# Token pairs in the q, k, v loads, no K copy, and an order planned around port and instruction fetch, in a one-core gated DeltaNet and MLP kernel

The kernel runs on one core of a Trainium2 chip. The metric is the device time of one execution in microseconds (us). Executions of the kernel before spread over some 3% on each chip, so every kernel was timed in alternation with it on the same chip. A ratio below is the mean time of one kernel's fast runs over the mean time of the other's fast runs of the same rounds, so it is not quite the ratio of the medians that stand beside it. "Fast" means no more here than within 1.5% of the fastest run that it was compared with.

## The reference

A gated delta rule over 768 tokens for 4 x 8 heads of 48 elements, then an MLP with a smooth ReLU on 3,072 tokens:

```python
def _attn_ref(q, k, v, beta, g):                    # (4, 8, 768, 48); beta (4, 8, 768)
    k_n = k / (np.linalg.norm(k, axis=-1, keepdims=True) + 1e-06)
    state = np.zeros((B, H, D, D))
    for t in range(S):
        y[:, :, t] = g[:, :, t] * np.einsum('bhd,bhde->bhe', q[:, :, t], state)
        v_old = np.einsum('bhde,bhd->bhe', state, k_n[:, :, t])
        state = state + beta_t * np.einsum('bhd,bhe->bhde', k_n[:, :, t], v[:, :, t] - v_old)
    return y

def _moe_ref(x, w_in, w_out):                       # (3072, 384), (384, 2048), (2048, 384)
    h = x @ w_in
    g = np.where(h >= 1, h, np.where(h <= -1, 0.0, (h + 1) ** 2 / 4))
    return g @ w_out
```

## The kernel before

Tokens are taken in 24 steps of 32, and four steps make a **group**. A group is prepared as a whole: load K, q and V; norm and scale; transpose on TensorE (PE); "grams" (K times K and q); mask; invert 128 small triangular matrices ("lanes": 14 rounds of two small operations); two merges. Then its four steps run one after another, each ending with a state update, and the finished group goes through the MLP. All instructions are first listed with an estimated duration and a priority. A planner simulates the engines and emits each engine's instructions in the order of its simulated start times.

```python
class Plan:
    def order(self):                      # a list scheduler with estimated durations
        ...
            if o["dma"] and not o["dma"][0]:
                done = end + 2.5          # a DMA with estimate 0 lands 2.5 us after its issue
        ...
        return [i for t, i in sorted(out)]
    def emit(self):
        for i in self.order():
            self.ops[i]["fn"]()
```

The parts that the change touches:

```python
def load(nm, g, prio, parts, ...):        # one token (192 B) per packet, 128 tokens on 128 partitions
    ... dma_start(out=t(g)[:, a:a + n], in_=whole(src, g, a, n)) ...
def beta_load():                          # 32 heads x 6 groups x 32 tokens: 768 pieces of 128 B
    a = bass.AP(..., ap=[[S, NH], [GS * C, NG], [1, C]])
def load_weights(prio):                   # input weights (win) in 16 pieces of 32 or 16 rows
    ... nc.gpsimd.dma_start(out=win[32 * h4 + p0:32 * h4 + p0 + n, kt, :], in_=moe_w_in[r0:r0 + n, :]) ...
def prep(g, ...):                         # K scaled into k, then copied beside V into pk
    ... tensor_tensor(out=ks(g)...) ... tensor_copy(out=spot(pk, D, a, n), in_=ks(g)...) ...
# order of work
lanes(g, t0 + 1.8 * T, ["POOL"] if g > 1 else ["DVE", "POOL"] if g else ["DVE"])
# (cut: merges, chain_step, mlp_in, mlp_out)
```

Of the kernel before, what the change touches and what calls it, by code (L numbers as in the profile page):

```python
# [22 lines left out]
class Plan:  # L23
# [8 lines left out]
    def add(self, eng, us, fn, r=(), w=(), prio=0.0, ninstr=0, dma=None, take=None, give=None, after=(), soon=0.0):  # L32
# [15 lines left out]
        self.ops.append(dict(eng=eng, us=us, fn=fn, deps=deps, prio=prio, n=ninstr, dma=dma, take=take, give=give, soon=soon))  # L48
        return i

    def order(self):
# [8 lines left out]
        fetch = [0, 0.0]  # L60
        dma = 0.0
# [16 lines left out]
        while len(out) < len(ops):  # L78
# [23 lines left out]
            p, i = heapq.heappop(now)  # L102
            o = ops[i]
            if o["take"]:
                c = o["take"][0]
                most, rest = self.limits[c]
                if held[c] >= most or len(spare) <= rest:
                    blocked.append((e, i))
                    continue
                held[c] += 1  # L110
                self.slot[o["take"]] = spare.pop(0)
            end = t + o["us"]
            if o["n"]:
# [36 lines left out]
def kernel(  # L150
# [17 lines left out]
    DM = H * D  # L168
    J = 8
# [5 lines left out]
    KW = 2 * D  # L175
    assert D == 48 and H == 8 and B == 4
# [17 lines left out]
    kraw = Ring("kraw", 1, [128, NH, D], FP)  # L194
    vraw = Ring("vraw", 1, [128, NH, D], FP)
    qraw = Ring("qraw", 1, [128, NH, D], FP)
    gs = Ring("g", 8, [128, J, D], FP)
    ksq = Ring("ksq", 1, [128, NH, D], FP)
    nsq, nrm, nre, rcp, rs = (Ring(n, 2, [128, NH], FP) for n in ("nsq", "nrm", "nre", "rcp", "rs"))
    ks = Ring("k", 1, [128, NH, 64], F16)  # L200
    qs = Ring("q", 1, [128, NH, 64], F16)
    pks = Ring("pk", 2, [128, 4, J, KW], F16)
# [3 lines left out]
    lts = Ring("lt", 1, [128, 32, 32], F16)  # L206
# [15 lines left out]
    gts = Ring("gt", 20, [128, NT], F16)  # L222
# [3 lines left out]
    sb = pool.tile([128, NG, NH], FP, name="sb")  # L226
# [20 lines left out]
    braw = pool.tile([128, NG, 32], FP, name="braw")  # L247
    bt = pool.tile([128, NG, NH], FP, name="bt")
# [10 lines left out]
    def P(eng, us, fn, r=(), w=(), prio=0.0, ninstr=0, dma=None, take=None, give=None, after=(), soon=0.0):  # L259
        plan.add(eng, us, fn, r, w, prio, ninstr, dma, take, give, after, soon)  # L260

    def whole(t, g, a=0, n=NH):

        return bass.AP(tensor=t.tensor, offset=t.offset + g * GS * C * D + a * S * D, ap=[[D, GS * C], [S * D, n], [1, D]])

    def load(nm, g, prio, parts, eng="SP", after=(), soon=0.0):
        t, src = dict(k=(kraw, k), q=(qraw, q), v=(vraw, v))[nm]
        e = {"SP": nc.sync, "ACT": nc.scalar}[eng]
        for a, n in parts:
            P(eng, 0.5, lambda a=a, n=n: e.dma_start(out=t(g)[:, a:a + n], in_=whole(src, g, a, n)),  # L270
              w=[t.key(g, a)], prio=prio, dma=(5.6 * n / NH, 128 * n), after=after, soon=soon)

    def load_g(s, prio, soon):
        for h4 in range(4):
            a = bass.AP(tensor=g_in.tensor, offset=g_in.offset + (2 * (h4 % 2) + h4 // 2) * S * D + s * C * D,
# [4 lines left out]
    def beta_load():  # L280
        for qd in range(4):
            a = bass.AP(tensor=beta.tensor, offset=beta.offset + qd * C, ap=[[S, NH], [GS * C, NG], [1, C]])
            P("ACT", 0.62, lambda p=32 * qd, a=a: nc.scalar.dma_start(out=braw[p:p + 32, :, :], in_=a),
              w=[("braw", qd)], prio=-120, dma=(0.0, 192))
# [5 lines left out]
    def setup():  # L290
# [13 lines left out]
        P("POOL", 1.9, diag, r=["ones"], w=["id32", "upf", "i128"], prio=-99)  # L304
        for rg in (ks, qs):
            for i in range(rg.n):
                P("DVE", 0.3, lambda i=i, rg=rg: nc.vector.memset(rg(i)[:, :, D:64], 0.0), w=[rg.key(i, "pad")], prio=-98)
        P("POOL", 0.9, lambda: nc.gpsimd.memset(lowl(0)[:], 0.0), w=[lowl.key(0, 0), lowl.key(0, 1)], prio=-40)
        P("POOL", 0.9, lambda: nc.gpsimd.memset(lowx(0)[:], 0.0), w=[lowx.key(0, 0), lowx.key(0, 1)], prio=-40)
# [7 lines left out]
        P("DVE", 0.4, lambda: nc.vector.transpose(out=bt[:].rearrange("p a b -> p (a b)"), in_=braw[:].rearrange("p a b -> p (a b)")),  # L317
          r=[("braw", n) for n in range(4)], w=["bt"], prio=-118)
        P("ACT", 0.36, lambda: nc.scalar.activation(out=sb[:].rearrange("p a b -> p (a b)"), in_=bt[:].rearrange("p a b -> p (a b)"), func=AF.Sqrt),
          r=["bt"], w=["sb"], prio=-118)  # L320

    def fill_bm(i, after=()):
# [3 lines left out]
        P("POOL", 2.7, f, r=["id32"], w=[bms.key(i, c) for c in range(GS)], prio=-55 + 20 * i, after=after)  # L326

    WIN = [("win", h4, kt, p0) for h4 in range(4) for p0, kt in ((0, 0), (0, 1), (16, 1), (0, 2))]

    def load_weights(prio):  # L330
        wp = win[:].ap[0][0]
        for h4 in range(4):
            for p0, kt, h2, e0, n in ((0, 0, 0, 0, 32), (0, 1, 0, 32, 16), (16, 1, 1, 0, 16), (0, 2, 1, 16, 32)):
                r0 = (h2 * 4 + 2 * (h4 % 2) + h4 // 2) * D + e0
# [84 lines left out]
    def ktk(g):  # L419
        return [kts.key(g, j) for j in range(J)]  # L420
# [304 lines left out]
```

## Time and profile before

| kernel before | |
|---|---|
| time, median of 4 runs beside the changed kernel | 335.99 us (332.31 to 341.31) |
| profiled run | 334.0 us, PE busy 242.6 us |
| first state update / that of step 4 / first MLP matmul | 44.3 / 93.8 / 91.3 us |
| PE idle before the first MLP matmul / after it | 58.0 / 33.3 us |

The shares of the engines and the busy time by stretch stand in the prediction. Two more views. First, the DMA view of the kernel before, from 0 to 20 us: 40 slices of 0.5 us, busy share of the 16 DMA engines in tenths, then GB/s.

```profile
DMA  0000999999999999997399999999999997000000
GB/s 0 0 0 17 200 256 252 184 200 243 250 198 252 245 218 214 237 233 122 66 224 261 255 193 249 244 238 235 219 216 218 218 218 113 0 0 0 0 0 0
```

From 2 to 17 us nearly all DMA engines work, mostly at 180 to 260 GB/s, with one dent to 66 GB/s. Second, two rows of the timeline of the kernel before, DVE and then PE; the brackets give the idle time before an instruction and what ended it.

```profile
7.41 0.38 DVE L317 STREAM_TRANSPOSE bt<-braw 128x192 f32<-128x192 f32 x1 [3.59 <-DMA braw<-in_beta_dram]
```
```profile
37.81 0.91 PE L498 MATMUL psn_158<-l_105,bm_97 32*32 32x32 f16 x52 [13.20 <-DVE l_105 L479]
```

Beta is there at 7.4 us, and the first merges start at 37.8 us, when DVE has inverted group 0.

### The profile page before, as it was taken

What the parts mean: (1) busy time and instruction counts of PE and PEld (TensorE: products, weight loads), DVE (VectorE), ACT (ScalarE), POOL (GpSimd) and SP (SyncE); (2) the same over time, 40 slices, a digit from 0 to 9 for tenths busy, and PEclk for the clock granted to TensorE, in tenths of its full rate; (3) what the DMA queues carried; (4) which work ended last, traced back from release to release, by engine and by line L of the source; (5) the groups of instructions that cost most, each with busy time, mean ns of one, the idle gap of its engine ahead of it and who ended that gap; (6) DMA issues with size and microseconds to landing.
All of it is one profiled execution on the core that took longest, in us unless ns stands there. A gap on an engine that the chain in (4) does not pass through costs nothing.

```text
span 334.0 us, 15565 instructions
## 1 busy us (share of the span) xinstructions
PE 242.6 (73%) x6960; PEld 149.6 (45%) x6960; DVE 212.9 (64%) x371; ACT 173.8 (52%) x300; POOL 165.7 (50%) x271
## 2 busy tenths in 40 slices
PE   0250364307678859797595997898997999899985
PEld 0140363206544436454363554555554555455443
DVE  3899922777677793774654676747538571985570
ACT  3430152004575637755386636587363764876871
POOL 8596091272625895478574158822485220332330
PEclk9999999999995878999669899589997899999999
DMA  8979699773388338645884343022110002001102
GB/s 174 213 135 192 109 162 211 150 154 81 68 160 168 76 69 166 136 108 116 185 167 103 74 113 68 10 69 58 49 49 4 6 3 73 27 3 48 48 0 94
DMA packets 112130, 32.56 MB, mean 97 GB/s; under 512 B 103488, under 2 KB 111680, under 8 KB 112064
## 3 DMA queue, kind: packets, MB, share of 16 engines
q1 hardware_dynamic: 104352, 27.54, 39.1%
q0 software_dynamic: 2752, 3.15, 6.0%
q10 hardware_dynamic: 4960, 0.89, 1.4%
q8 instruction: 54, 0.88, 1.1%
q14 instruction: 12, 0.10, 0.1%
HBM read 25.26 MB, written 4.72 MB: 90 GB/s over the span
## 4 chain that ended last, share of the span: by engine, by line
PE 43%; DVE 20%; POOL 13%; issue 12%; ACT 5%; DMA 4%; ACTq 1%; SPq 1%; DVEq 0%; POOLq 0%
POOL lm_101 L469 5%; POOL tm_102 L466 5%; PE psn_162 L602 3%; DVE lt_100 L447 3%; PE psn_160 L629 3%; PE psn_158 L602 2%; PE psn_159 L602 2%; PE psn_159 L629 2%; PE psn_163 L602 2%; DVE lm_101 L469 2%; DVE tm_102 L466 2%; PE psn_160 L602 2%; DMA out_dram<-ot_151 2%; PE psn_161 L602 2%; PE psn_161 L629 2%
## 5 line engine op out<-in xcount | busy, mean ns | idle before, releaser
L602 PEld LDWEIGHTS <-win 128*128 128x128 f16 x288 | 26.4, 103 | 28.7 <-issue 7.3
L615 POOL TENSOR_TENSOR rl_127<-rl_127 128x512 f32<-128x512 f32 x12 | 12.5, 1040 | 34.1 <-ACT rl_127 L605 34.1
L615 POOL TENSOR_TENSOR rl_126<-rl_126 128x512 f32<-128x512 f32 x12 | 13.2, 1098 | 32.6 <-ACT rl_126 L605 32.6
L469 POOL TENSOR_TENSOR lm_101<-lm_101,tm_102 128x28 f32<-128x28 f32 (+13 forms) x70 | 24.6, 351 | 5.5
L466 POOL TENSOR_TENSOR tm_102<-lt_100,lm_101 128x28 f32<-128x28 f16 (+13 forms) x70 | 23.7, 338 | 5.1
L615 POOL TENSOR_TENSOR rl_128<-rl_128 128x512 f32<-128x512 f32 x12 | 12.9, 1077 | 18.2 <-ACT rl_128 L605 18.2
L457 POOL TENSOR_SCALAR lm_101<-lt_100 128x512 f32<-128x512 f16 (+1 forms) x5 | 6.9, 1385 | 26.8 <-DVE lt_100 L447 21.0
L408 PEld LDWEIGHTS <-k_83 128*128 128x128 f16 x96 | 11.5, 121 | 17.1 <-DVE k_83 L367 16.1
L566 ACT CAST s_120<-sps 128x768 f16<-128x768 f32 x11 | 8.8, 800 | 13.9 <-PE sps L563 13.8
L566 ACT CAST s_119<-sps 128x768 f16<-128x768 f32 x12 | 9.7, 808 | 8.9 <-PE sps L563 8.9
L367 POOL TENSOR_TENSOR k_83<-kraw_61,rs_82 128x768 f16<-128x768 f32 x6 | 8.8, 1484 | 9.9 <-DVE rs_82 L365 9.9
L408 PE MATMUL psn_158<-i_169,k_83 128*128 128x128 f16 x24 | 5.2, 263 | 11.1 <-DVE k_83 L367 10.6
L409 PEld LDWEIGHTS <-q_84 128*128 128x128 f16 x96 | 11.6, 121 | 3.2 <-issue 1.6
L385 POOL CAST q_84<-qraw_63 128x768 f16<-128x768 f32 x10 | 8.7, 880 | 6.5 <-DMA qraw_63<-in_q_dram 6.1
L375 POOL TENSOR_TENSOR pk_85<-vraw_62,sb 128x768 f16<-128x768 f32 x6 | 8.9, 1475 | 4.9 <-DMA vraw_62<-in_v_dram 3.8
L498 PEld LDWEIGHTS <-bm_97 32*32 32x32 f16 x256 | 4.2, 111 | 15.6 <-issue 15.6
L356 ACT ACTIVATE ksq_72<-kraw_61 128x768 f32<-128x768 f32 x12 | 10.0, 840 | 2.4 <-issue 1.5
L501 ACT CAST e_109<-psn_158 128x512 f16<-128x512 f32 x2 | 1.2, 586 | 19.2 <-PE psn_158 L498 19.2
L498 PE MATMUL psn_158<-l_105,bm_97 32*32 32x32 f16 x64 | 1.1, 227 | 13.2 <-DVE l_105 L479 13.2
L367 POOL TENSOR_TENSOR k_83<-kraw_61,rs_81 128x768 f16<-128x768 f32 x4 | 5.9, 1472 | 9.1 <-DVE rs_81 L365 9.1
L602 PE MATMUL psn_162<-xt_124,win 128*128 128x512 f16 x30 | 9.4, 429 | 0.0
L375 POOL TENSOR_TENSOR pk_86<-vraw_62,sb 128x768 f16<-128x768 f32 x6 | 8.9, 1504 | 1.1 <-DMA vraw_62<-in_v_dram 1.1
(591 smaller groups left out, 861.2 us busy)
## 6 DMA issues: line engine op xcount, KB each, us to landing
kraw_61<-in_k_dram SPq DMA_DIRECT2D x12, 384.0 KB, 4.0
qraw_63<-in_q_dram SPq DMA_DIRECT2D x12, 384.0 KB, 6.3
vraw_62<-in_v_dram SPq DMA_DIRECT2D x10, 384.0 KB, 5.8
wout<-in_moe_w_out_dram POOLq DMA_DIRECT2D x4, 384.0 KB, 8.7
out_dram<-ot_151 SPq DMA_DIRECT2D x8, 192.0 KB, 1.9
out_dram<-ot_152 SPq DMA_DIRECT2D x8, 192.0 KB, 1.9
out_dram<-ot_153 SPq DMA_DIRECT2D x8, 192.0 KB, 1.9
win<-in_moe_w_in_dram POOLq DMA_DIRECT2D x8, 128.0 KB, 5.8
```

The lines of the kernel that those rows point to most:

```text
L356: P("ACT", 0.25 + 1.3 * f, lambda hs=hs: nc.scalar.activation(out=ksq(g)[:, hs], in_=kr[:, hs], func=AF.Square), r=[kraw.key(g, a)], w=[ks ...
L367: P(eng, (0.15 + 1.65 * f) if eng == "DVE" else (0.2 + 2.8 * f), lambda hs=hs, a=a, n=n, eng=eng: EW[eng].tensor_tensor(out=ks(g)[:, hs, 0 ...
L375: P(eng, (0.15 + 1.65 * f) if eng == "DVE" else (0.2 + 2.8 * f), lambda hs=hs, a=a, n=n, eng=eng: EW[eng].tensor_tensor(out=spot(pk, 0, a, ...
L408: nc.tensor.matmul(tp[:, hh, 0], kk[:, o:o + 128], i128[:], start=(hh == 0), stop=True, skip_group_check=True)
L409: nc.tensor.matmul(tp[:, hh, 1], qq[:, o:o + 128], i128[:], start=False, stop=True, skip_group_check=True)
L447: P("DVE", 1.95, lambda: nc.vector.transpose(out=lt[:].rearrange("p i j -> p (i j)"), in_=_ap(bm, [[1, 32], [64, 32]])), r=[bms.key(gi, c) ...
L466: e.tensor_tensor(out=tv, in0=_ap(lt, [[528, nb], [32, n], [0, j]], 32 * (j + 1) + j + ot), in1=_ap(lm, [[256, nb], [0, n], [1, j]], 16 * ...
L469: e.tensor_tensor(out=lv, in0=lv, in1=tv, op=ALU.subtract)
L566: P("ACT", 0.8, lambda: nc.scalar.copy(out=s16n[:].rearrange("p a j d -> p a (j d)"), in_=sps[:, :, 0:J * D]), r=["sps"], w=[s16s.key(s)], ...
L602: nc.tensor.matmul(hp, win[:, kt_, m * 128:m * 128 + 128], xt[:, kt_].rearrange("p b t -> p (b t)"), start=(kt_ == 0), stop=(kt_ == 2))
L615: P("POOL", 1.05, lambda: nc.gpsimd.tensor_tensor(out=rl[:], in0=rl[:], in1=rl[:], op=ALU.mult), r=[rls.key(i)], w=[rls.key(i)], prio=prio)
L629: nc.tensor.matmul(bv(n, DM), gts(gi * NM + m)[:, b * GS * C:(b + 1) * GS * C], wout[:, m, :], start=(m == 0), stop=(m == NM - 1))
```

## The change

The intent: a packet of q, k or v carries two neighbouring tokens (384 B instead of 192 B). K is scaled straight into its place beside V, so the copy goes. Group 1's lanes leave DVE. Later groups are prepared up to three steps earlier. The planner keeps VectorE's two-port work apart from GpSimd's, and fills with MLP matmuls where it believes that the next block of instructions is not there yet. Along with that, the input weights are loaded in fewer, larger DMAs and beta in larger packets. The planner's transfer estimate for a whole K, q or V was lowered too, from 5.6 to 3.5 us. The core of the diff:

```diff
+            if e == "PE" and fetch[0] + ops[i]["n"] >= 256 and fetch[1] + 3.4 > t + 0.3:
+                few = [x for x in now if 0 < ops[x[1]]["n"] <= 8 and not self.full(x[1], held, spare)]
+                ...                                   # take the MLP matmul first
+            if o["port"]:
+                end = max(t, port[e == "DVE"]) + o["us"]
+                port[e == "POOL"] = end
 ...
-    kraw = Ring("kraw", 1, [128, NH, D], FP)
+    kraw = Ring("kraw", 1, [128, 2 * J, TP, D], FP)    # TP = 2 tokens
 ...
-            a = bass.AP(tensor=beta.tensor, ..., ap=[[S, NH], [GS * C, NG], [1, C]])
+            a = bass.AP(tensor=beta.tensor, ..., ap=[[0, 2], [2 * S, 2 * J], [1, S - x]])
 ...
-        for h4 in range(4):
-            for p0, kt, h2, e0, n in (...): ...        # 16 input-weight DMAs
+        parts = [(win[:, 0, :], [[D * DFF, 4], [DFF, 32], [1, DFF]], 0, 128), (win[:, 2, :], [[D * DFF, 4], [DFF, 32], [1, DFF]], ..., 128)]
+        for h4 in range(4):
+            parts.append((win[32 * h4:32 * h4 + 32, 1, :], [[160 * DFF, 2], [DFF, 16], [1, DFF]], ..., 32))
 ...
-            P("DVE", ..., tensor_copy(out=spot(pk, D, a, n), in_=ks(g)...))
+                P(eng, ..., lambda: EW[eng].tensor_tensor(out=<K's place in pk>, in0=raw, in1=scale, op=ALU.mult), port=True)
 ...
-        lanes(g, t0 + 1.8 * T, ["POOL"] if g > 1 else ["DVE", "POOL"] if g else ["DVE"])
+        lanes(g, t0 + 1.8 * T, ["POOL"] if g else ["DVE"])
+    PRE = 3.0                                          # groups 2 to 5 prepared 3 steps earlier
```

## The prediction

> **What bounds the kernel now.** I read the page first: the busy shares of the engines, then the span in 40 slices.
>
> ```profile
> PE 242.6 (73%) x6960; PEld 149.6 (45%) x6960; DVE 212.9 (64%) x371; ACT 173.8 (52%) x300; POOL 165.7 (50%) x271
> ...
> PE   0250364307678859797595997898997999899985
> ...
> DMA  8979699773388338645884343022110002001102
> ```
>
> No engine is busy throughout, but the PE row has two halves: poorly filled for about eleven slices, and 70 to 90% and more after. So I asked for the busy time in stretches, cut at 91 us, where the first matmul of the MLP (line 602) stands. The columns are the stretch and its length, then busy time with counts for PE, weight loads, DVE, ACT and POOL, the granted clock, the DMA share and GB/s.
>
> ```profile
> 0.00:91.00 91.00, 32.95 (x1512) 27.99 (x1516) 60.71 (x134) 26.46 (x48) 50.22 (x89) 1.00 0.83 150
> 91.00:334.00 243.00, 209.66 (x5456) 121.63 (x5456) 152.16 (x238) 147.30 (x252) 115.50 (x183) 0.90 0.35 78
> ```
>
> This is the account I shall use: span = PE busy + PE idle. In the first 91 us PE idles 91 - 33 = 58 us; in the other 243 us it idles 33 us. After 91 us PE has the MLP as filler. At the end it even has a stock of it: the last state update (line 563) is at 288 us, and PE runs MLP matmuls almost without a hole until 331 us, when two groups of MLP, about 2 x 21 us, were still to do (16 x 0.65 us on line 602 and as much on line 629, durations from the chain of work). So a shorter recurrence does not by itself shorten the end. What counts is how early PE gets MLP work, and how many holes it has after.
>
> Where do the 58 us go? The timeline of DVE between 12 and 20 us, then POOL in the same time (start, duration, engine, line, operation):
>
> ```profile
> 12.53 3.12 DVE L362 TENSOR_SCALAR nre_77<-nrm_75 128x16 f32<-128x16 f32 x1 [0.28 <-ACT nrm_75 L360]
> ...
> 16.79 2.18 DVE L367 TENSOR_TENSOR k_83<-kraw_61,rs_81 128x768 f16<-128x768 f32 x1
> 19.00 1.11 DVE L370 COPY pk_85<-k_83 128x768 f16<-128x768 f16 x1
> ```
> ```profile
> 12.40 1.48 POOL L375 TENSOR_TENSOR pk_85<-vraw_62,sb 128x768 f16<-128x768 f32 x1 [3.79 <-DMA vraw_62<-in_v_dram]
> 13.82 1.80 POOL L324 MEMSET bm_98<- 128x2048 f16 x1
> ```
>
> The same DVE operations on the first half of K took 0.17, 0.96 and 0.36 us. Here 16 elements take 3.12 us and end exactly when POOL's memset does (15.65 against 15.62). The excess is 2.95 + 0.61 (line 365: 0.78 for 0.17) + 1.22 + 0.75 = 5.5 us, all on the chain.
>
> Then PE's own timeline, the idle time in brackets:
>
> ```profile
> 54.25 0.51 PE L434 MATMUL psn_158<-kt_95 48*32 48x64 f16 x23
> 59.23 0.32 PE L434 MATMUL psn_158<-kt_95 48*32 48x64 f16 x9 [4.47 <-issue]
> ...
> 73.84 0.51 PE L554 MATMUL psn_159<-rr_115,z_112 32*32 32x48 f16 x32 [10.02 <-DVE rr_115 L542]
> ```
>
> The 4.47 us hole lies in the middle of 32 equal matmuls, with nothing to wait for. Counted in the timeline, such holes in mid-block (at 42.01, 46.56, 52.76, 59.23) are 128 matmuls apart, which is 256 instructions with the weight loads: instruction fetch. The page counts 54 instruction packets of 0.88 MB; 13,920 PE instructions over 256 gives the same 54. Up to 91 us the chain of work holds seven such pieces: 1.02 + 1.83 + 1.27 + 4.47 + 0.74 + 2.29 + 0.64 = 12.3 us. The longest falls into the stretch 50 to 60 us, where the DMA share was 1.27. The 10.02 us hole is step 2 waiting for one DVE subtraction, queued behind half of group 1's triangular inverse ("lanes", lines 457 to 475), which ran on DVE from 62 to 73 us. Before that, group 0's lanes took DVE from 27.4 to 36.6 us.
>
> **What the Trainium skill says.** "GPSIMD Engine Reference", Specifications: its SBUF interfaces are shared with VectorE, with contention for DVE instructions in a 2-port mode or with two SBUF inputs. The 3.12 us row agrees; the lanes, with two SBUF inputs each, also stretch from 0.21 to 0.33 us while POOL runs its half. "Runtime: NRT & Kernel Launch", Instruction fetch mechanics: blocks of 16 KiB, 256 instructions, fetched ahead by DMA, the cost "mostly hidden". The block size agrees; mostly hidden it is not here (12.3 us before 91). "DMA: Bandwidth & Descriptors", Specifications: line rate wants at least 512 B. Now q, k, v rows are 192 B each, and the page has 103,488 of 112,130 packets under 512 B at 97 GB/s on average; 384 B is better and still under the mark. "TensorE: Matmul & The Clock Gate", Part 1: 128-column matmuls run 107 ns apart cold and about 56 warm. The trace agrees: line 408 and 409 go every 0.11 us at 47 us and every 0.06 us at 94 us.
>
> **The change part by part.**
>
> Token pairs. A packet carries two tokens. q, k, v need 6 groups x 3 x 4096 = 73,728 packets now, half that after, out of the 104,352 on that queue. The queue's 39.1% share of 334 us is 131 us; if its packets cost alike, 36,864 fewer save 36.9/104.4 x 131 = 46 us of mean DMA time. Almost all is hidden after 91 us; in the start it brings K, then V, a few us earlier and frees the path for instruction fetch. Beta goes from 768 packets to 128; today DVE waits for it until 7.41 us (3.6 us idle).
>
> K copy dropped. Line 370 goes: 12 copies, 5.2 + 3.0 = 8.2 us of DVE; of it 0.36 to 1.11 us in group 0 on the chain. The transposes now read K where it lies beside V, so they wait for V as well, and K needs two 64-column matmuls where one of 128 stood: 16 more per group, 96 in all. If they do not overlap in the array, 96 x 0.055 = 5 us more PE time; I expect some overlap and take 4. Norms go in one piece after group 0, saving about 0.6 us of small DVE operations (lines 362, 364, 365: 0.17 + 0.25 + 0.17) in each of 5 groups, off the path.
>
> Port-aware order. Group 0's K chain should lose nearly all of the 5.5 us. Beta and V earlier, and no issue of V's load on ACT (ACT's squares stood from 8.67 to 10.42 behind it), are worth 2 to 3 us more: step 0, whose first matmul is at 43.0, comes at about 35.
>
> Lanes of group 1 on POOL alone. DVE is free between 62 and 73 us, so steps 1 to 3 do not wait 10 us. The price: POOL needs some 28 x 0.345 + 1.4 + 0.95 + 0.57 = 12.6 us for a whole group (rows of lines 466, 469, 457, 472, 475), so step 4 is set by the path V and K scaling, transposes, grams, lanes, two merges. From 36 us, the earliest that the code allows, with 6 us of POOL scaling, about 4.5 for transposes, 5.5 for grams, masks and the transpose, 13 for lanes, 6 for the rest, that is about 72 us, against 93 now. Steps 0 to 3 need 3.9 us each undisturbed (L554 at 73.84 and 77.68), here with group 1's work between, perhaps 7: from 35 to about 62. First MLP matmul at about **64 us, not 91**.
>
> Fetch-aware order. Where the next block isn't there, MLP matmuls (8 instructions or fewer for 0.65 us) go first. It can only help where MLP exists. After 91 us the chain's pieces of fetch over 0.7 us sum to 1.85 + 0.79 + 1.53 + 0.78 + 2.07 = 7.0; I credit 5. Fewer holes should also leave fewer cold matmuls (triples on line 602 that take 1.39 us for 0.65): credit 3 us of busy time.
>
> Loads and preparation three steps earlier, 19 for 20 MLP buffers, fewer weight DMAs: hidden, 0.
>
> **Sum.** Early idle: by 64 us PE will have done about 28 us of work (the 33 less group 1's merges and the transposes of group 2), so it idles 36 us instead of 58. Late idle: 33 - 5 = 28. Busy: 242.6 + 4 - 3 = 243.6. Together 36 + 28 + 243.6 = 307.6, say **308 us**: 8% off.
>
> **Rivals.** (a) *POOL becomes the bound in the middle.* It takes all lanes of group 1, and three prepared groups at a time compete for it; if group 1's lanes end at 75 us rather than 66, PE uses up MLP group 0 and stands idle until step 7 is done. For it: 58 us busy in 91 to 180 already. Against it: 0.5 of the span in all, and each group's MLP is 21 us of filler. It would cost 8 to 12 us: 318. (b) *The 58 us aren't won because instruction fetch, not data, paces the start.* 54 blocks at a few us each are serial; more matmuls, closer together, wait at each boundary, with no filler before the MLP. For it: 12.3 us today. Against it: DMA is emptier. First MLP then at 74: 318. (c) *The gain is larger.* If PE stays warm in the middle (mean granted clock after 91 us is 0.90, so up to 21 us are there to win) and the late idle falls to 20, the result is near 295. (d) *DMA hidden anyway.* The packets alone would give nearly nothing after 91 us; I count on them only for the start.
>
> **Range and chances.** The sum has 22 us from the early idle (likely 14 to 32), 8 from fetch and clock (0 to 18), -4 for the extra matmuls (-6 to 0). Combined, 295 to 321. The three runs of the kernel before spread from 332.3 to 341.3, so run noise is small beside this. Slower or same needs rivals (a) and (b) both and more: faster by over 2% 0.93, within 0.06, slower 0.01.
>
> **What would show it.** Right: first matmul of the MLP near 64 us; no DVE operation of 16 elements over 0.5 us in the first 20 us; first state update near 36; no 10 us hole at step 2; q, k, v packets halved; PE's idle time before the first MLP about 36 us and after it about 28. Wrong: MLP still starting after 75 us; a PE hole after the first MLP group with POOL's lanes as the releaser; fetch holes in mid-block as long as before; PE busy time above 250 from the 192 half-width K matmuls.

## More of the kernel before

Most kernels have 4 runs, beside few of the kernel before; e8 has 12, and e3, e5, e12, e13 and e17 have 20. Set against all runs of the kernel before that the record calls fast on that chip, the 4-run ratios shift: e1 from 1.028 to 1.037, e16 from 1.045 to 1.056, e18 from 1.023 to 1.034, e15 from 1.011 to 1.006. So differences of about a point are weak where a kernel with 4 runs is one of the two.

## The result, and the profile after

| | before | after |
|---|---|---|
| median (4 runs each) | 335.99 us | 349.75 us (346.20 to 351.24) |
| ratio after to before, 95% interval | | 1.0482 [1.0329, 1.0635] |
| profiled run | 334.0 us | 349.4 us |
| first state update / that of step 4 / first MLP matmul | 44.3 / 93.8 / 91.3 us | 62.3 / 118.5 / 101.0 us |
| PE busy / idle before the first MLP matmul / idle after it | 242.6 / 58.0 / 33.3 us | 242.3 / 71.6 / 35.5 us |

The result is correct and **4.8% slower**, with 308 us predicted. The ratio rests on the two runs of the kernel before that lie within 1.5% of its fastest (332.31 and 334.01 us); over all four the means differ by 3.8%. A repeat on another chip (e16 below) gave 1.0447. From the page of the changed kernel: busy shares, PE and DMA in 40 slices, all packets, then the load queue.

```profile
PE 242.3 (69%) x7056; PEld 150.7 (43%) x7056; DVE 194.6 (56%) x313; ACT 175.8 (50%) x297; POOL 163.5 (47%) x259
...
PE   0027005234376854689897889989898999899986
...
DMA  5569978993897396376740223421321002001102
...
DMA packets 76074, 32.85 MB, mean 94 GB/s; under 512 B 67304, under 2 KB 75496, under 8 KB 76008
...
q1 hardware_dynamic: 71684, 28.52, 41.4%
```

PE's busy time has not changed. It starts one slice later, its fifth and sixth slices are empty, and until the eleventh it is busy for half of a slice or less but for one slice (70%). The queue of the loads has 71,684 packets instead of 104,352, but its share of the span rose: 41.4% of 349.4 us is 145 us of mean DMA time, where it was 131 us. The busy time in two stretches, cut at the first MLP matmul, columns as in the prediction:

```profile
0.00:101.00 101.00, 29.37 (x1272) 25.02 (x1272) 42.56 (x92) 27.16 (x51) 44.29 (x66) 0.91 0.88 148
101.00:349.40 248.40, 212.96 (x5786) 125.71 (x5784) 152.04 (x221) 148.69 (x247) 119.21 (x194) 0.89 0.33 72
```

PE idles 101.0 - 29.4 = 71.6 us in the first stretch, 13.6 us more than before, and 35.4 us in the second, 2.1 more. Together, less 0.3 us of busy time, that is the 15.4 us by which the profiled runs differ. So the loss lies before the first MLP matmul. The DMA view of the changed kernel, 0 to 20 us, in the same slices as before:

```profile
DMA  0000075999999411148995111116999311116997
GB/s 0 0 0 0 25 111 140 302 221 149 194 227 190 76 38 28 38 106 197 297 176 73 26 43 25 55 57 174 255 236 122 44 45 42 41 36 118 253 309 148
```

Three times the DMA engines fall to a tenth of their time and the rate to some 25 to 57 GB/s: from 7 to 8.5, 11 to 13.5 and 16 to 18 us. What then stands still is seen in the timeline of the changed kernel, DVE first, then POOL, then PE:

```profile
17.52 0.25 DVE L341 STREAM_TRANSPOSE bt_164<-braw 128x64 f32<-128x64 f32 x1 [15.16 <-DMA braw<-in_beta_dram]
...
34.74 1.75 DVE L387 TENSOR_REDUCE nsq_74<-ksq_72 128x32 f32<-128x1536 f32 x1 [1.76 <-ACT ksq_72 L385]
36.41 1.89 DVE L483 STREAM_TRANSPOSE lt_99<-bm_96 128x1024 f16<-128x1024 f16 x1
```
```profile
24.43 2.92 POOL L404 TENSOR_TENSOR pk_84<-vraw_62,sb 128x768 f16<-128x768 f32 x2 [16.19 <-DMA vraw_62<-in_v_dram]
...
75.11 1.60 POOL L413 CAST q_83<-qraw_63 128x768 f16<-128x768 f32 x2 [14.67 <-DMA qraw_63<-in_q_dram]
```
```profile
22.30 0.61 PE L437 MATMUL psn_157<-i_169,q_83 128*128 128x128 f16 x4 [22.30 <-ACT q_83 L411]
...
51.74 0.96 PE L534 MATMUL psn_161<-l_105,bm_96 32*32 32x32 f16 x56 [17.71 <-DVE l_105 L515]
...
75.99 0.61 PE L437 MATMUL psn_159<-i_169,q_83 128*128 128x128 f16 x4 [12.71 <-POOL q_83 L413]
```

Three things can be read here. **Beta comes at 17.5 us instead of 7.4**, and V at 24.4 us. **Work of later groups stands in front of earlier work**: at 34.74 DVE reduces the norms of group 1 (nsq_74), having waited for them, before it transposes group 0's masks, which were complete at 33.0 us. At 75.99 PE has waited 12.7 us for the q of group 2, while the matmuls of step 1 stand behind that instruction. And the input weights came late. The list of DMA issues has the size of each and the median time from issue to landing, the kernel before first, then the changed one:

```profile
win<-in_moe_w_in_dram POOLq DMA_DIRECT2D x8, 128.0 KB, 5.8
```
```profile
win<-in_moe_w_in_dram POOLq DMA_DIRECT2D x2, 512.0 KB, 21.0
...
win<-in_moe_w_in_dram POOLq DMA_DIRECT2D x4, 128.0 KB, 20.0
```

Pieces of the same 128 KB took 5.8 us before and 20.0 us after. In the same lists a half of K takes 4.0 us from issue to landing before and 8.1 us after, while the plan assumed less time than before.

### The profile page after: what moved, and what is told of

Read it like the earlier page. It is cut to its first block, busy times and chain, and to the rows that moved or that the text cites.

```text
span 349.4 us, 15681 instructions
## 1 busy us (share of the span) xinstructions
PE 242.3 (69%) x7056; PEld 150.7 (43%) x7056; DVE 194.6 (56%) x313; ACT 175.8 (50%) x297; POOL 163.5 (47%) x259
## 3 DMA queue, kind: packets, MB, share of 16 engines
q1 hardware_dynamic: 71684, 28.52, 41.4%
## 4 chain that ended last, share of the span: by engine, by line
PE 41%; issue 4%; DVE 4%; ACT 4%; DMA 2%; SPq 2%; POOL 1%; DVEq 0%; POOLq 0%; ACTq 0%
PE psn_157 L669 4%; PE psn_162 L669 3%; PE psn_159 L669 3%; PE psn_160 L639 3%; PE psn_158 L639 3%; PE psn_161 L639 2%; PE psn_160 L669 2%; PE psn_161 L669 2%; PE psn_157 L639 2%; PE psn_162 L639 2%; PE psn_159 L639 2%; PE sps L597 2%; SPq L299 1%; PE psn_161 L546 1%; DMA g_70<-in_g_dram 1%
## 5 line engine op out<-in xcount | busy, mean ns | idle before, releaser
L655 POOL TENSOR_TENSOR rl_126<-rl_126 128x512 f32<-128x512 f32 x12 | 12.9, 1078 | 56.9 <-ACT rl_126 L642 56.9
L505 POOL TENSOR_TENSOR lm_101<-lm_101,tm_102 128x28 f32<-128x28 f32 (+6 forms) x70 | 26.0, 372 | 5.5
L437 PEld LDWEIGHTS <-q_83 128*128 128x128 f16 x96 | 8.2, 127 | 36.6 <-ACT q_83 L411 22.3
L655 POOL TENSOR_TENSOR rl_127<-rl_127 128x512 f32<-128x512 f32 x12 | 12.5, 1042 | 22.0 <-ACT rl_127 L642 21.9
L655 POOL TENSOR_TENSOR rl_128<-rl_128 128x512 f32<-128x512 f32 x12 | 12.5, 1041 | 17.1 <-ACT rl_128 L642 17.1
L437 PE MATMUL psn_157<-i_169,q_83 128*128 128x128 f16 x20 | 3.0, 307 | 22.7 <-ACT q_83 L411 22.3
L404 POOL TENSOR_TENSOR pk_85<-vraw_62,sb 128x768 f16<-128x768 f32 x6 | 9.3, 1560 | 15.3 <-DMA vraw_62<-in_v_dram 12.3
L502 POOL TENSOR_TENSOR tm_102<-lt_100,lm_101 128x28 f32<-128x28 f16 (+6 forms) x42 | 14.5, 345 | 2.6
L413 POOL CAST q_83<-qraw_63 128x768 f16<-128x768 f32 x8 | 6.4, 833 | 14.7 <-DMA qraw_63<-in_q_dram 14.7
L385 ACT ACTIVATE ksq_72<-kraw_61 128x1536 f32<-128x1536 f32 (+1 forms) x7 | 9.0, 1295 | 8.2 <-DMA kraw_61<-in_k_dram 8.2
L437 PE MATMUL psn_159<-i_169,q_83 128*128 128x128 f16 x28 | 3.8, 282 | 12.9 <-POOL q_83 L413 12.7
L404 POOL TENSOR_TENSOR pk_85<-kraw_61,rs_82 128x768 f16<-128x768 f32 x6 | 9.5, 1593 | 4.3 <-DVE rs_82 L394 4.3
L502 POOL TENSOR_TENSOR tm_102<-lt_99,lm_101 128x28 f32<-128x28 f16 (+6 forms) x28 | 10.2, 364 | 1.7
L639 PE MATMUL psn_157<-xt_123,win 128*128 128x512 f16 x33 | 10.6, 436 | 0.0
L404 POOL TENSOR_TENSOR pk_84<-kraw_61,rs_81 128x768 f16<-128x768 f32 x4 | 6.4, 1614 | 6.9 <-DVE rs_81 L394 6.8
L341 DVE STREAM_TRANSPOSE bt_164<-braw 128x64 f32<-128x64 f32 x3 | 0.7, 246 | 15.5 <-DMA braw<-in_beta_dram 15.2
```

What stands on the lines that cost most here:

```text
L385: P("ACT", 0.2 + 1.3 * f, lambda js=js: nc.scalar.activation(out=ksq(g)[:, js], in_=kr[:, js], func=AF.Square), r=raw(kraw, g), w=over(ksq ...
L404: P(eng, (0.15 + 1.65 * f) if eng == "DVE" else (0.05 + 2.9 * f), lambda o=o, eng=eng: EW[eng].tensor_tensor(**o()), r=raw(raw_, g) + (ove ...
L413: P("POOL", 0.05 + 1.6 * f, lambda o=o: nc.gpsimd.tensor_copy(**o()), r=raw(qraw, g), w=over(qs.key, a, n), prio=prio)
L437: nc.tensor.matmul(tp[:, x, c], qq[:, c, j * 128:j * 128 + 128], i128[:], start=(x == 0 and c == 0), stop=True, skip_group_check=True)
L502: e.tensor_tensor(out=tv, in0=_ap(lt, [[528, nb], [32, n], [0, j]], 32 * (j + 1) + j + ot), in1=_ap(lm, [[256, nb], [0, n], [1, j]], 16 * ...
L505: e.tensor_tensor(out=lv, in0=lv, in1=tv, op=ALU.subtract)
```

## The experiments

Two theories were formed from this. **N (narrow transfers)**: the Trainium skill, "DMA: Bandwidth & Descriptors", section "Why a DMA increments its semaphore by 16 and not by 1", under "How many engines (k)", says that a DMA is spread over the largest k up to 16 that divides the slowest dimension (that is not 1) of both sides. The new beta pattern has slowest dimension 2, the new weight pieces 4 or 2. The trace agrees: at times when only beta's packets were being moved, 2.1 to 2.2 packets were in flight on average, against about 20 when K was. The new beta is also larger: 64 packets of 3,072 B and 64 of 2,816 B (368 KB), where 768 packets of 128 B were 96 KB. At the 35 to 41 GB/s of those stretches, 368 KB take some 9 to 11 us (an estimate). **Q (queue order)**: each engine's order is that of the planner's estimates, and where these are far off, work of later groups blocks an engine until its data comes. The rivals are those of the prediction (POOL, instruction fetch), and **C**: PE's cold clock gives gains back.

All kernels below give correct results except e4. Two times stand for how far a kernel has come: the first state update (step 0, the first of group 0) and that of step 4 (the first of group 1).

### e1, e2, e3: wide transfers

e1 takes beta with 32 rows as the slowest dimension, e2 the input weights in 16 pieces as before, e3 both. The instruction order of e3 was compared with that of the changed kernel and is the same but for the added DMA issues.

```diff
-            a = bass.AP(tensor=beta.tensor, offset=beta.offset + h4 // 2 * S + x, ap=[[0, 2], [2 * S, 2 * J], [1, S - x]])
+            a = bass.AP(tensor=beta.tensor, offset=beta.offset + x, ap=[[S, NH], [1, S - x]])
 ...
-        parts = [...]                                  # 2 + 4 DMAs, slowest dimension 4 or 2
+            for p0, kt, row, n in ((0, 0, h4 * D, 32), (0, 1, h4 * D + 32, 16), (16, 1, (4 + h4) * D, 16), (0, 2, (4 + h4) * D + 16, 32)):
+                ... out=win[32 * h4 + p0:32 * h4 + p0 + n, kt, :], in_=moe_w_in[row:row + n, :] ...
```

> The changed kernel with one edit: each of the four beta loads takes all 32 heads as 32 rows (slowest dimension 32) instead of 16 rows read twice (slowest dimension 2); the wanted half is picked by the two square roots behind it. Bytes, descriptor sizes and the order of work on every engine stay the same. Theory N (narrow transfers): a transfer whose slowest dimension is 2 runs on 2 of the 16 DMA engines, so beta, 4 x about 92 KB, lands at 17 us; with 32 rows it lands by 8 to 10 us, the first transposes come at 13 to 15 instead of 22.3 us, and the time falls by 6 to 9 us, to 341 to 344. Rival O (order: work of later groups put ahead of its data blocks the engines): the start is paced by K, q and V as before, the time stays within 2 us of 350. Rival P (the 384-byte packets to 64 partitions are slow): beta lands late still, since K and q hold the engines; within 2 us.

> The changed kernel with one edit: the first MLP weight is loaded in 16 pieces of 32 or 16 rows (slowest dimension 32 or 16) instead of 6 pieces whose slowest dimension is 4 or 2. Order of work the same on every engine but for the added issues on POOL. Theory N: those loads land in about 6 us instead of 20, the second group of k/v rows (10.7 us from issue to landing) and the instruction fetches near 42 to 50 us are no longer behind them; gain 3 to 8 us, to 342 to 347. Rivals O and P: the weights are needed at 101 us only, no gain, within 2 us of 350.

> The changed kernel with both edits, wide beta and wide MLP weight. Theory N alone: the whole loss is undone and some of the forecast gain appears, 325 to 336. If N is right but only half of the cause, the hole of 12.7 us on PE before group 2's q transposes (63 to 76 us) stays, since that transfer was issued only at 60.7 us, and the time is 336 to 343: then the order (O) holds the rest. P alone: 348 to 352.

Measured: e1 1.0277 [1.0195, 1.0359], e2 1.0256 [1.0157, 1.0355], e3 1.0177 [1.0135, 1.0219]. The mechanism of N holds: in e1 beta is there at 8.67 us; in e2 weight pieces land in 5.4 us. By the ratios each is worth about 2 points against the 1.048 and 1.045 of the changed kernel, both together about 3. All three times missed what N expected (e3: 344.8 us, not 325 to 336). And e1's gain did not come as N said: its first state update is at 71.6 us, later than the 62.3 of the changed kernel, while steps 1 and 4 are earlier (81.6 for 85.0, 114.7 for 118.5). This is e1's DVE timeline:

```profile
37.32 1.75 DVE L387 TENSOR_REDUCE nsq<-ksq 128x32 f32<-128x1536 f32 x1 [12.55 <-ACT ksq L385]
38.99 1.89 DVE L483 STREAM_TRANSPOSE lt<-bm 128x1024 f16<-128x1024 f16 x1
```

Group 0's masks were complete at 24.8 us, 8 us earlier than in the changed kernel. Yet DVE stood for 12.55 us at the norms of group 1, whose K was issued at 19.3 us and came late beside the narrow weight loads. The transpose of the masks, ready all the time, ran at 38.99, later than the 36.41 of the changed kernel. Q is seen here in one row. The planner, printed by itself, has beta's transpose at 4.54 us (measured 17.5), this reduction at 22.24 and the mask transpose at 23.99 (measured 36.41): in the plan K of group 1 was there in time, and the reduction had the higher priority.

### e4: the narrow transfers in the kernel before

Both kinds of transfer of the kernel before made narrow (the expectation names beta alone), its order otherwise its own. The result is wrong (relative error 0.05), as rows go to other places.

```diff
-            a = bass.AP(..., offset=beta.offset + qd * C, ap=[[S, NH], [GS * C, NG], [1, C]])
+            a = bass.AP(..., offset=beta.offset + qd * C, ap=[[S, 2], [2 * S, 16], [1, NG * C]])
 ...                                                   # and the 2 + 4 weight DMAs of the change
```

> The kernel before with one edit: its four beta loads have the same bytes, in 32 rows of 768 B in the order 2 x 16 (slowest dimension 2) instead of 32 x 6 pieces of 128 B. The result is wrong on purpose. Order of work unchanged. Theory N: beta runs on 2 engines and lands at 11 to 15 us instead of 7.4, the first transposes move by as much, and the time grows by 3 to 8 us, to 338 to 343. Rivals O and P: fewer and larger packets can only help, within 2 us of 335.

Measured: 1.0197 [1.0087, 1.0307]. Slower, as N says, but its trace doesn't show the loss where N puts it. Beta comes at 8.41 us (1 us later), the first state update at 45.2 (0.9 later), step 4 at 96.9 (3.1 later). PE idles 1.4 us more before the first MLP matmul, but 6.7 us more after it, and is 3.6 us longer busy. But this beta is still 96 KB, a quarter of the changed kernel's, so e4 tests a narrow beta without the added bytes; at 35 to 41 GB/s it takes less than 3 us (an estimate). That width and bytes together do harm in an order that is not the changed kernel's, e14 below shows. Where e4's 2% comes from is not settled.

### e5, e6, e7: group 0 first, no early preparation

e5 is e3 with group 1's norms (DVE) and scaling (POOL) ordered behind group 0's lanes. e6 is e3 with PRE = 0. e7 has both.

```diff
-  r=over(ksq.key, a, n), w=over(nsq.key, a, n), prio=prio)
+  r=over(ksq.key, a, n), w=over(nsq.key, a, n), prio=prio, after=[lowx.key(0, 0)] if g == 1 else ())
 ...                                                   # the same after= on the K and V scaling
-    PRE = 3.0
+    PRE = 0.0
```

> Wide loads (as e3) and one change of order: group 1's norm (DVE) and its K and V scaling (POOL) come after group 0's triangular inverse. In e3 DVE stood 5.9 us waiting for group 1's K ahead of group 0's transpose of the masks, then 1.75 us for that norm, and the inverse took 12.4 us beside POOL's scaling against 8.3 before. Theory O (work of later groups put ahead): the first update of the state comes at 52 to 56 instead of 66 us, the first MLP matmul at 82 to 88 instead of 92.5, and the time falls to 332 to 340. Rival F (DMA and fetch bound start): the gained time turns into longer instruction-fetch holes and waits for loads between 45 and 65 us, the time stays at 341 to 346.

> Wide loads (as e3) and PRE = 0: loads and preparation of groups 2 and later are not put three steps earlier in the order. Theory O, second part: group 2's q and K loads no longer share 45 to 65 us with the weights and no longer stand on PE before step 1; steps 1 to 3 come 4 to 8 us earlier and the time falls by 2 to 8 us, to 336 to 342. If early preparation is worth what it was meant to be, later groups are late instead and the time grows to 346 to 352.

> Wide loads with both changes of order (e5 and e6). Theory O: gains add, 326 to 336, faster than the kernel before. Rival F: no better than the better of the two.

Measured: e5 1.0084 [1.0050, 1.0119], e6 1.0468 [1.0387, 1.0549], e7 1.0373 [1.0283, 1.0463]. The first part of Q holds: the first state update moves from 66.0 us (e3) to 48.8, earlier than expected, and about a point is won (343.3 us, not the expected 332 to 340). My suspicion of early preparation as such does not: without it, both kernels lose nearly 3 points. In e5, PE next stands at

```profile
62.89 0.61 PE L437 MATMUL psn<-i,q 128*128 128x128 f16 x4 [6.49 <-POOL q L413]
```

again group 2's q ahead of step 1, whose state update comes only at 69.6 us.

### e8, e11: group 2 behind group 1

e8 is e7 with PE's transposes of later groups placed behind the masks of the group before, and the output weights loaded later. e11 has only the first of the two.

```diff
+              ... take=n, after=[bms.key(g - 1, c) for c in range(GS)] if g > 1 else ())
 ...
-              after=[l16s.key(0)], w=[("wout", i)], ..., soon=38.0)
+              after=[l16s.key(0)], w=[("wout", i)], ..., soon=60.0)
```

> As e7, and two more: group 2 and later transposes on PE only after the group before has its masks, and the second MLP weight (3.1 MB, wanted at about 100 us) is held back to a planned 60 us instead of 38. Theory F: DMA has less to carry between 45 and 65 us, fetch holes there shrink from 3.9 and 5.4 us to under 2.5, time 2 to 6 us under e7. Theory O alone: within 3 us of e7, as the rest of the order is the same.

> e7_g0_first_pre0 (352.8, ratio 1.0373) with only the one order change that PE takes group 2's transposes after group 1's masks; the output weights still load early. Between e7 and e8 3.8 points lie. If blocked PE queue is their cause (Q): ratio 1.00 to 1.01, second state update near 61 instead of 69.8. If the early load of the output weights, which shares DMA with instruction fetch, is the cause: ratio stays above 1.025.

Measured: e8 **0.9995 [0.9947, 1.0043]**, e11 1.0299 [1.0206, 1.0391]. With width and order repaired, the change is as fast as the kernel before. Between e7 and e8 lie 3.8 points; the transposes account for 0.7 and the output weights for the other 3. The same 42 matmuls in PE's timeline, e11 first, then e8:

```profile
62.54 0.77 PE L470 MATMUL psn<-kt 48*32 48x64 f16 x42 [5.42 <-issue]
```
```profile
59.04 0.77 PE L470 MATMUL psn<-kt 48*32 48x64 f16 x42 [3.61 <-issue]
```

With the early load, e11's PE stands 5.42 us in mid-block, without a wait, and then 4.23 us for a K/V transfer at 68.0. In e8 the first wait is still 3.61 us, where under 2.5 was expected, and the second is gone; the first state updates follow at 49.4, 60.9, 67.8 and 72.1 us and the first MLP matmul at 75.4, 16 us earlier than in the kernel before. That these 16 us are worth nothing is taken up below. In e8's DVE timeline, at the start:

```profile
8.40 0.37 DVE L341 STREAM_TRANSPOSE bt<-braw 128x64 f32<-128x64 f32 x2 [6.05 <-DMA braw<-in_beta_dram]
...
14.51 4.53 DVE L404 TENSOR_TENSOR pk<-kraw,rs 128x384 f16<-128x384 f32 x4
```

Even wide and in order, K's scaling ends at 19.0 us, as in the kernel before (16.79 + 2.18): the four operations take 4.53 us, as POOL scales V from 15.28 to 18.63. In the changed kernel, where V was late, the same four took 1.96 us.

### e9, e10, e12, e15: single parts of the change, in the repaired order

Each differs from e8 in one thing: PRE back at 3.0 (e9); group 1's lanes split over DVE and POOL as in the kernel before (e10); the fetch rule off (e12); the port rule off (e15).

```diff
-    PRE = 0.0
+    PRE = 3.0                                                                    # e9
-        lanes(g, t0 + 1.8 * T, ["POOL"] if g else ["DVE"])
+        lanes(g, t0 + 1.8 * T, ["POOL"] if g > 1 else ["DVE", "POOL"] if g else ["DVE"])   # e10
-            if e == "PE" and fetch[0] + ops[i]["n"] >= 256 and ...
+            if False and ...                                                     # e12
-            if o["port"]:
+            if False:                                                            # e15
```

> The kernel of e8_all_order (339.0 us, ratio 0.9995) with early preparation put back (three steps ahead for groups 2 to 5). Theory Q (work of later groups that stands ahead of earlier work in an engine's queue, waiting for its own data, causes the loss): with those blocks now placed after the earlier group's work, early preparation no longer blocks and helps as in e3 against e6 (2.9 points): 330 to 334 us, ratio 0.97 to 0.985. Rival C (the time is set by PE's warm-up and total queue length, early preparation only moves work): no gain, ratio 0.99 to 1.01. First state updates in both: 49, 61, 68, 72.

> e8_all_order with group 1's triangular inverse split again, one half on DVE and one on POOL, as in the kernel before. Rival (a) of the prediction (POOL bounds the middle): e8's step 4 (94.8 us) comes at about 86 and the ratio falls from 0.9995 to about 0.98. Theory Q: step 4 comes earlier, but MLP of group 0 fills PE meanwhile and DVE delays steps 1 to 3: within 0.5 per cent of e8.

> e8_all_order without the rule that puts MLP matmuls ahead where the planner believes that the next instruction block is not there. The prediction credited the rule with 5 us of idle and 3 of clock (2.4 per cent): then 347, ratio 1.02. Theory Q has nothing on it; the planner's block times (3.4 us each) seldom hit the real holes, so I expect within 0.7 per cent of e8.

> e8_all_order with the planner no longer keeping POOL work and DVE's two-port work apart. The prediction valued that at 5.5 us in the start: then step 0 comes about 4 to 6 us later and the ratio is 1.01 to 1.02. Rival: in e8's trace the K scaling on DVE already runs beside POOL's V scaling (4.53 us for 1.96), so the rule holds only in the plan, not on the chip: within 0.7 per cent of e8.

Measured: e9 1.0201 [1.0141, 1.0260], e10 1.0233 [1.0148, 1.0318], e12 1.0039 [1.0004, 1.0073], e15 1.0111 [1.0056, 1.0166].

- e9 missed its expectation of 0.97 to 0.985. At 79.2 us PE again waits 5.59 us for a later group's K scaling on POOL, step 4 comes at 105.3 instead of 94.8. Early preparation helped e3 and hurts e8, so these edits do not add up.
- e10: lanes on POOL alone are the better choice, by 2.4 points. Split, step 3 comes at 82.8 us instead of 72.1, and step 4 at 103.6 instead of 94.8. Rival (a) finds no support here: giving half of the lanes back to DVE doesn't bring step 4 earlier.
- e12: the fetch rule is worth 0.4 points, and the intervals of e8 and e12 overlap; I had credited 2.4%.
- e15: the port rule gives about 1 point by the ratio, 0.6 against all fast runs of the kernel before on that chip, so its size is not settled. It is not where I had put it: e15's K scaling in the start takes 4.53 us like e8's, and its first state update comes at 49.4.

### e13: three more places

Group 1's norms behind group 0's transposes of the inverse, group 2's behind group 1's mask transpose, the output weights' issue (3.11 us on POOL) out of group 1's lanes.

```diff
+  ... after=[x16s.key(0)] if g == 1 else [lts.key(g - 1)] if g else ())
-              ... soon=60.0)
+              ... soon=84.0)
```

> e8_all_order with three more blocks moved behind the work they stand in front of: group 1's norm (1.75 us) behind the two transposes of group 0's inverse, group 2's norm (1.75 us) behind the transpose of group 1's masks, the issue of the output weights (3.11 us on POOL) behind group 1's inverse. Theory Q: step 0 comes 1.7 us and step 4 some 5 us earlier (94.8 to about 89), PE idles 3 to 5 us less, ratio 0.985 to 0.99 (331 to 334 us). Rival C (PE's cold clock and the filling of PE after the first MLP give it back, as in e8, where 11 us of early idle became nothing): ratio 0.995 to 1.005 although step 4 is earlier.

Measured: 335.92 us, **0.9948 [0.9915, 0.9980]**. This is the best version found: half a per cent under the kernel before, which by the 2% mark is still the same, and about 5% under the change as it was. Step 0 comes 1.3 us earlier (1.7 were expected); step 4, expected at about 89 us, comes at 95.3.

### e14: the order alone

The order of e8, with the changed kernel's own narrow beta and weights.

> The kernel after with the order repaired as in e8_all_order, but with its own narrow beta and input-weight transfers. Theory N (the narrow transfers cost their delay at the start, whatever the order): step 0 some 8 us later than in e8, ratio 1.025 to 1.035. Rival: if the order alone was the cause and the widths only shift hidden work, ratio 1.00 to 1.01.

Measured: 1.0318 [1.0239, 1.0396], from two fast runs of four; beta at 15.95 us, first state update at 56.2, step 4 at 103.7. N holds in the repaired order too: there the widths are worth about 3 points. Both repairs alone leave a loss (1.018 and 1.032); together they leave none.

### e16, e17, e18: repeat, one step early, loads later

e16 is the changed kernel again. e17 is e13 with PRE = 1.0. e18 is e13 with group 2's K, q and V loads held back until after 62 us in the plan.

```diff
-    PRE = 0.0
+    PRE = 1.0                                                                    # e17
-            load("k", g + 1, t0 if g else -99)
+            load("k", g + 1, t0 if g else -99, soon=62.0 if g == 1 else 0.0)     # e18, q and v alike
```

> The changed kernel itself, unchanged, for a ratio on the same chip as e17 and e18. All theories: 1.03 to 1.06, as the 1.048 measured first.

> e13_three_more with preparation one step ahead for groups 2 to 5 instead of none. If early preparation only hurts by standing ahead of earlier work (Q), one step is short enough to do no harm and gives step 8 and later ones their data earlier: ratio 0.985 to 0.995. If any early preparation takes PE's and POOL's time from the steps that need it: 1.00 to 1.01.

> e13_three_more with the K, q and V loads of group 2 issued after about 62 us instead of from 53 us. In e13 the holes without a wait at 57 and 61 us were 2.81 and 1.98 us while these loads ran. Rival (b) as the prediction put it (fetch has a pace of its own): they stay at 2 to 3 us, ratio as e13 or worse. If fetch waits behind the loads' packets: both shrink below 1 us, the first MLP matmul comes 3 to 4 us earlier (72 to about 68); group 2's preparation may give that back, so the ratio lies between 0.985 and 1.00.

Measured: e16 1.0447 [1.0347, 1.0548]; e17 1.0098 [1.0063, 1.0134]; e18 1.0226 [1.0151, 1.0301]. For rival (b), the same ten matmuls of step 1, e13 first, then e18, in PE's timeline:

```profile
57.17 0.24 PE L616 MATMUL psn<-u,bm 32*32 32x48 f16 x10 [2.81 <-issue]
```
```profile
55.46 0.30 PE L616 MATMUL psn<-u,bm 32*32 32x48 f16 x10 [0.34 <-issue]
```

Between 50 and 55 us the DMA share was 1.30 in e13 and 0.32 in e18. With the loads away, this hole shrinks from 2.81 to 0.34 us; the next one only from 1.98 to 1.72, against my "both below 1 us". The waits return elsewhere (one of 4.47 us at 103.9 us), and the kernel is slower. This fits a fetch that waits in part behind the loads, on one execution of each; moving the loads moved the holes. In e17 even one step of early preparation costs 1.5 points more than e13 in this order, and step 4 comes at 100.4 us instead of 95.3.

## Why the prediction was wrong

The account "span = PE busy + PE idle" held. Most of the error is early idle time, although having less of it did not shorten the span by itself (5). The sum had 36 us early idle, 28 late and 243.6 busy; measured were 71.6, 35.5 and 242.3. The 42 us of error are 35.6 early, 7.5 late and -1.3 busy.

1. **The step that failed first**: "A packet carries two tokens ... in the start it brings K, then V, a few us earlier", with "Beta goes from 768 packets to 128". I counted packets. (a) In the first 25 us a packet of 384 B takes 22 to 34 ns (medians of the runs), one of 192 B takes 15, so packets cost by bytes here; the 46 us saved on the queue were in fact 14 us more (131 to 145). By packet size, q, k and v together took about 72 us of that queue's time before (an estimate: 69,632 packets at the mean of 16.5 ns, over 16 engines) and 72.3 us after; most of the 14 us are the 1,536 B packets (31.1 to 39.1) and the 4 B ones (2.5 to 5.1). From 4 to 14 us e8, with wide loads, moves some 180 to 270 GB/s, no more than the kernel before outside its dent. (b) Beta's 128 packets carry nearly four times the bytes, on two DMA engines. Beta came at 17.5 us, where I had expected it before 7.4. e1 (beta at 8.67 when wide) and e14 against e8 show it. I had listed "fewer weight DMAs" as "hidden, 0"; they were narrow as well, and e2 shows them worth some 2 points.

2. **"Port-aware order ... step 0, whose first matmul is at 43.0, comes at about 35."** Step 0's first matmul came at 58.0. The port clash of the kernel before was gone in the changed kernel only because V was late; with V early it came back (4.53 us, e8), with the rule or without it (e15). Even repaired, step 0 comes at about 45.8 (e8), later than the 43.0 of the kernel before. Waits for fetch of 2.27 us just before it and 2.39 us within it are part of that.

3. **A step that I left out.** I took it that moving work earlier in the plan costs nothing where it is not ready. In an in-order queue it blocks: 12.71 us at 75.99 in the changed kernel, 12.55 us in e1, 6.49 in e5. I put preparation "three steps earlier" down as hidden, 0. In e8's order it costs 2 points (e9), in e3's it gains 3 (e6): its worth depends on what it is put in front of. Together, 1 to 3 turned "first MLP matmul at about 64 us" into 101.

4. **Lanes on POOL**: the choice was right (e10), the size too small (and the terms for step 4 add to 71, not 72). I had 12.6 us; in e8 they take from 64.83 to 83.1 us, less the 3.11 us of the weights' issue inside, so 15.2. "Step 4 at about 72" was 118.5 in the changed kernel and 94.8 repaired.

5. **"What counts is how early PE gets MLP work."** This failed even for the repaired kernel. e8 starts the MLP at 75.4 us, not 91.3, and idles 11.1 us less before; yet it ends 3.7 us later in the profile.

| profiled run | step 4 | first MLP | PE idle before it | PE busy, all | PE idle after it | last update | span |
|---|---|---|---|---|---|---|---|
| before | 93.8 | 91.3 | 58.0 | 242.6 | 33.3 | 288.0 | 334.0 |
| after | 118.5 | 101.0 | 71.6 | 242.3 | 35.5 | 302.6 | 349.4 |
| e14 order only | 103.7 | 86.2 | 58.6 | 248.0 | 36.5 | 296.2 | 343.1 |
| e8 width and order | 94.8 | 75.4 | 46.9 | 251.3 | 39.5 | 290.9 | 337.7 |
| e13 three more | 95.3 | 71.9 | 44.7 | 246.3 | 40.3 | 284.5 | 331.3 |

The last state update stands 46 to 47 us before the end in every one of the 20 profiles: two groups of MLP always follow it. So the end is set by when the recurrence is through, and "A shorter recurrence does not by itself shorten the end" did not hold in these profiles. But e8's recurrence is through 3 us later than that of the kernel before (290.9 against 288.0), although the MLP starts 16 us earlier. The packed traces, with PE's busy time cut at step 4 and at the last update, say where the gain went.

- Before step 4, which is no earlier in e8 (94.8 against 93.8), PE has done 18 MLP matmuls instead of 6, only 4.4 us more of MLP work, and between the first of them and step 4 it idles 6.4 us (kernel before: 0). The 6.2 us more of idle time after the first MLP matmul lie there.
- Between step 4 and the last update PE idles no more than before (27.9 us against 28.6), so missing MLP filler is not the cause. MLP takes 2.5 us less there (103.3 against 105.8), but the recurrence's own matmuls, 4,610 instead of 4,560, take 74.1 us instead of 69.2.

Step 4 alone doesn't decide the end either: e18 has it at 93.0 us and ends 10 us after the kernel before, and the time from step 4 to the last update is 184 to 205 us in the 20 profiles.

PE's busy time is 4 to 9 us longer in the repaired kernels. In e8 6.3 us of it are recurrence matmuls, 2.2 output matmuls and 0.3 input matmuls. The 96 additional matmuls were 5 us at most by the prediction; in the changed kernel, which has them too, PE is not longer busy (242.3 us). The rest may be C: the Trainium skill, "TensorE: Matmul & The Clock Gate", Part 1, says that PE runs at half clock until it has been busy for a window of about 3.4 us. The clock records agree (all stretches but the last are multiples of 3.4 us, at 1.0 or 0.5), and between step 4 and the last update the mean clock was 0.83 in e8 against 0.88 in the kernel before. But the profiles of e8 and e12, which differ in the fetch rule alone, have 251.3 and 246.4 us, so how much of it is chance is not settled, and C as the cause is not shown.

6. **Fetch**: I credited 5 + 3 us. Off against on is 0.4 points, within the noise (e12), and I had assumed that MLP would exist early enough to fill. Rival (b) has a part: e8's holes without a wait before the MLP sum to 11.9 us, as much as the 12.3 that I had counted in the kernel before, and depend on DMA only in part (e18).

What stays open: why e4 loses 2% mainly after the first MLP matmul; why the order edits do not add up (e3 to e6, e5 to e9); why the recurrence takes longer after step 4 in e8, so that the repaired change gains nothing; and what it would take to bring step 4 earlier, as e13 did not.

## What to carry to other kernels

Before counting packets, look at the slowest dimension and at the bytes of each new access pattern: a "larger" transfer on two engines can hold up everything behind it. When a planner emits in-order queues, compare its assumed landing times with the trace first, and look for instructions of later work that wait just ahead of ready ones; a row with a long wait whose follower was ready is the sign. And let filler work be judged by what comes after it: in e8 it starts 16 us earlier, and the end, which the recurrence sets, comes no earlier.

## What the Trainium skill lacked or had wrong

- "DMA: Bandwidth & Descriptors": its rule on k agreed, and was there to be read before the prediction. What the page does not say there is the cost: for k = 2, 2.1 to 2.2 packets in flight and 35 to 41 GB/s, against about 20 packets and 180 to 270 GB/s for wide loads (e8). And its mark of 512 B (Specifications) doesn't tell what a larger packet below it is worth: doubling the packet gained nothing here, with a mean of 16.5 ns for 192 B in the kernel before and 31.4 ns for 384 B in the changed one, and 180 to 270 GB/s in e8 against 180 to 260 before.
- "Runtime: NRT & Kernel Launch", Instruction fetch mechanics, calls the cost of a block boundary mostly hidden. Here single mid-block waits of up to 5.42 us (e11), put down to fetch because they stand 128 matmuls apart, stood on PE's path, and one fell from 2.81 to 0.34 us when the loads beside it were taken away (e18).
- "TensorE: Matmul & The Clock Gate" agreed, with stretches of n x 3.4 us. No page says that the profile shows a clock of 1.0 up to its first record (93.6 us in the kernel before, 79.1 us in the changed one), while 128-column matmuls go every 0.11 us at 47 us in the kernel before and every 0.06 us at 94 us.
- No page has what an instruction costs that is put into an in-order queue ahead of its data: here 12.55 and 12.71 us in single rows.
